# Loading q in 4352-byte runs, with q and FFN columns in blocks of 32 tokens and a new issue order, in an attention-plus-FFN kernel

## The chip, the cores and the metric

The kernel runs on one core of one Trainium2 chip. The time is the device time of that core, in microseconds (us). One number is a median over several executions. A run is called slow when it is over 1.5% above the fastest run of the same kernel; ratios use fast runs only. Engines in the profile: PE (matmul), PEld (PE's weight loads), DVE (VectorE), ACT (ScalarE), POOL (GpSimd), SP (SyncE, which issues most DMAs; a "q" after an engine name means its sequencer, where issues and waits are shown).

## The reference

Inputs are q, k, v of shape (4 batches, 4 heads, 1088 tokens, 32), small matrices S1, S2 (8 x 32), and FFN weights. All is fp32 at the interface.

```python
def phi(x):                                   # 64 features per token and head
    a = np.einsum('rd,bhsd->bhsr', S1, x)
    b = np.einsum('rd,bhsd->bhsr', S2, x)
    return np.einsum('bhsi,bhsj->bhsij', a, b).reshape(*x.shape[:-1], r * r)
q_p, k_p = phi(q), phi(k)
kv  = np.einsum('bhsf,bhsd->bhfd', k_p, v)    # one small matrix per batch and head
z   = np.sum(k_p, axis=2)
x   = (q_p @ kv) / (q_p . z + 1e-6)           # attention output, heads joined: 128 columns
# FFN on x, with the previous token mixed in
xk  = mu_k * x + (1 - mu_k) * x_prev
xr  = mu_r * x + (1 - mu_r) * x_prev
out = sigmoid(xr @ w_r) * (relu(xk @ w_k) ** 2 @ w_v)     # 128 -> 1024 -> 128
```

All K of a batch must be summed before any q of that batch can be used. So the start of the kernel is: load K and V of batch 0, sum them, fold the sum with S, then project q, then the FFN. From there on, K sums of later batches run between FFN work of earlier ones.

## The kernel before

The kernel is written as small named operations with an explicit issue order (ORDER). `KT` transposes K, `KP` projects it, `KF` makes the products kp, `KA` adds up kv on PE, `KD` folds the sum; `QT`, `Q1`, `QF`, `QR`, `QX` do the same for q; `M1`, `RE`, `SQ`, `M2` are the FFN, `FN` multiplies by the sigmoid and stores. `Z/n` are n dummy matmuls that keep PE busy. `/DVE`, `/ACT` name the engine, `/b3` the PSUM bank.

The parts that the change and the argument touch:

```python
hdq = [const.tile([P, U, 2, D], F32, name=f"hdq{b}") for b in range(B)]

def load_k(b, eng):                            # 4352-byte runs
    eng.dma_start(hdk[b][:], k[b].rearrange("h (a c u) d -> (h a) c u d", a=32, c=2))

def load_q(b, engs):                           # 4 DMAs a batch, 256-byte runs
    for h in range(H):
        engs[h % len(engs)].dma_start(hdq[b][32 * h:32 * h + 32].rearrange("a t c d -> a t (c d)"),
                                      q[b, h].rearrange("(t a c) d -> a t (c d)", a=32, c=2))
# ... all loads are issued at once on SyncE, batch by batch
load_k(0, nc.sync)
# ... S1, S2, mu_k, mu_r on ScalarE
load_v(0, nc.sync)
load_q(0, [nc.sync])
for b in range(1, B):
    load_k(b, nc.sync)
    load_v(b, nc.sync)
    load_q(b, [nc.sync])
# ... weights, on GpSimd's queue
nc.gpsimd.dma_start(wk[:], moe_w_k)
nc.gpsimd.dma_start(wr_f[:], moe_w_r)
nc.gpsimd.dma_start(wv[:], moe_w_v.rearrange("(c p) d -> p c d", p=P))

GS = [2, 2, 4, 4, 4, 4, 4, 4, 4, 2]            # groups of 128-token tiles
parts = [(0, 2), (2, n)] if n == 4 else [(0, 3), (3, n)]      # each K sum in two parts

def fin(g):                                    # one output DMA per group, 128 partitions
    n = GS[g]
    o = work.tile([P, 4, P], F32, name="osb", tag="osb", bufs=4)
    nc.vector.tensor_mul(flat(o[:, :n]), tiles[f"o_{g}"][:, :n * P], rs[g][:, :n * P])
    nc.sync.dma_start(orow[G0[g] * P:(G0[g] + n) * P].rearrange("(t p) f -> p t f", p=P), o[:, :n])
```

## Time and profile before

| | before |
|---|---|
| time, median of 3 runs | 98.54 us (97.06 to 99.57) |
| span of the profiled run (which took 97.5 us) | 95.7 us |
| first K product on DVE starts | 9.37 us |
| last product on DVE ends | 91.96 us |
| from there to the end of the span (the tail) | 3.71 us |

Lines from the page of the kernel before. The first numbers are busy time, share of the span and instruction count. The rows of digits cut the span into 40 slices: busy tenths per engine, PE's granted clock in tenths (PEclk), DMA engines' busy tenths, and GB/s. The DMA queue lines give packets, megabytes and share of the engines' time. The last of these lines is a DMA group with its issue count, size of each and time to landing.

```profile
span 95.7 us, 3103 instructions
PE 84.5 (88%) x1285; PEld 57.5 (60%) x1285; DVE 79.6 (83%) x187; ACT 69.5 (73%) x161; POOL 5.6 (6%) x24
...
PE   5969898498849999999999999999999999999920
...
DVE  4073974989278999999799999989999999999840
...
PEclk9999999999999999999999999999999999999997
DMA  2999999999999999000010300340000030030422
GB/s 66 264 226 181 226 180 199 178 232 199 202 163 250 245 181 138 10 0 0 0 55 7 110 7 0 110 116 0 0 0 0 7 98 15 0 110 0 116 83 81
DMA packets 17773, 9.70 MB, mean 101 GB/s; under 512 B 10704, under 2 KB 17104, under 8 KB 17760
...
PE 34%; DMA 22%; ACT 18%; DVE 13%; SPq 6%; issue 3%; DVEq 1%; ACTq 0%
...
hdq<-in_q_dram SPq DMA_DIRECT2D x16, 136.0 KB, 7.3
```

After slice 12 (29 us) PE and DVE are full. Before it, DVE has holes and the DMA row stands at 9 up to slice 16, 38 us. More than half the packets are under 512 bytes, most of them q. The chain of work that ended last spends 22% in DMA. The list of waits of the same kernel (engine, line, what it waited for; us in total, times, longest) names loads among the waits of VectorE:

```profile
DVE St L247 <- DMA S<-in_S_dram: 3.2, 1, 3.2
...
DVE kT L310 <- DMA hdk<-in_k_dram: 2.3, 1, 2.3
```

And the group that stores the output (durations of an issue are minimum, median and maximum in ns):

```profile
L562 SPq DMA_DIRECT2D out_dram<-osb x10: 372/372/952, 34.6 to 92.1; - x10
```

### The profile page before, as it was taken

To read this page: it belongs to the slowest core of one execution; us is meant where nothing else is said; L and a number is where in the kernel's file an instruction comes from. 1 tells how busy PE (TensorE), PEld (TensorE's weight loads), DVE (VectorE), ACT (ScalarE), POOL (GpSimd) and SP (SyncE) were. 2 spreads that over 40 slices of the span, in tenths; PEclk is the share of its full clock that TensorE was granted. 3 is DMA by queue.
4 is the path that set the end of the run, shared out by engine and by line. 5 is a ranking of instruction groups with operands and counts; after the bars stand their busy time and mean duration, and the time that the engine had idled before them with its cause. 6 is when DMAs were issued, how large, how long until landed. Compare 5 with 4: busy or idle time off the path is not lost.

```text
span 95.7 us, 3103 instructions
## 1 busy us (share of the span) xinstructions
PE 84.5 (88%) x1285; PEld 57.5 (60%) x1285; DVE 79.6 (83%) x187; ACT 69.5 (73%) x161; POOL 5.6 (6%) x24
## 2 busy tenths in 40 slices
PE   5969898498849999999999999999999999999920
PEld 1316556464637668787567588876459636748910
DVE  4073974989278999999799999989999999999840
ACT  0622101379928879899999999568999999999900
POOL 6005400050000000000000000000000000000000
PEclk9999999999999999999999999999999999999997
DMA  2999999999999999000010300340000030030422
GB/s 66 264 226 181 226 180 199 178 232 199 202 163 250 245 181 138 10 0 0 0 55 7 110 7 0 110 116 0 0 0 0 7 98 15 0 110 0 116 83 81
DMA packets 17773, 9.70 MB, mean 101 GB/s; under 512 B 10704, under 2 KB 17104, under 8 KB 17760
## 3 DMA queue, kind: packets, MB, share of 16 engines
q1 hardware_dynamic: 16224, 8.92, 45.6%
q0 software_dynamic: 1216, 0.59, 4.5%
q8 instruction: 10, 0.16, 0.7%
q10 hardware_dynamic: 320, 0.00, 0.2%
q14 instruction: 3, 0.02, 0.1%
HBM read 7.80 MB, written 2.23 MB: 105 GB/s over the span
## 4 chain that ended last, share of the span: by engine, by line
PE 34%; DMA 22%; ACT 18%; DVE 13%; SPq 6%; issue 3%; DVEq 1%; ACTq 0%
DMA hdk<-in_k_dram 15%; ACT k L515 9%; PE ps_h L507 8%; PE ps_o L536 7%; DMA hdq<-in_q_dram 6%; SPq L169 6%; PE ps_kv L345 4%; PE ps_abw L420 3%; PE ps_x L480 3%; ACT PP L489 3%; ACT k L526 3%; DVE k L524 3%; DVE XK L494 3%; PE ps_qtp L465 3%; PE ps_kab L317 2%
## 5 line engine op out<-in xcount | busy, mean ns | idle before, releaser
L515 ACT ACTIVATE k<-ps_h 128x512 bf16<-128x512 f32 (+1 forms) x66 | 32.1, 577 | 0.7 <-PE ps_h L507 0.6
L507 PE MATMUL ps_h<-XK,wk 128*128 128x512 bf16 (+1 forms) x80 | 21.6, 349 | 0.4 <-DVE k L517 0.2
L536 PE MATMUL ps_o<-wv,k 128*128 128x128 bf16 x272 | 18.9, 219 | 0.1
L536 PEld LDWEIGHTS <-k 128*128 128x128 bf16 x272 | 16.3, 98 | 3.5 <-issue 0.8
L524 DVE TENSOR_TENSOR k<-k 128x1024 bf16<-128x1024 bf16 (+1 forms) x25 | 14.8, 618 | 0.4 <-ACT k L515 0.4
L526 ACT ACTIVATE k<-k 128x1024 bf16<-128x1024 bf16 (+1 forms) x15 | 13.7, 922 | 0.0
L300 DVE TENSOR_TENSOR kp<-ab 128x512 f32<-128x512 f32 (+1 forms) x16 | 11.5, 744 | 1.5 <-ACT ab L286 1.5
L465 PE MATMUL ps_qtp<-ident,qp 128*128 128x128 f32 x68 | 9.9, 277 | 1.6 <-DVE qp L300 1.6
L300 DVE TENSOR_TENSOR qp<-an,ps_abw 128x512 f32<-128x512 f32 x17 | 11.0, 679 | 0.1
L286 ACT COPY qpT<-ps_qtp 128x512 f32<-128x512 f32 (+1 forms) x17 | 8.5, 544 | 2.1 <-PE ps_qtp L465 2.0
L465 PEld LDWEIGHTS ps_qtp<-ident,qp 128*128 128x128 f32 x68 | 7.6, 141 | 4.1 <-issue 1.5
L507 PEld LDWEIGHTS <-wk 128*128 128x128 bf16 x80 | 6.7, 97 | 5.3 <-issue 2.5
L243 PE MATMUL wt<-zero 128*128 128x512 bf16 x24 | 8.4, 498 | 1.2 <-DVE warm L156 1.2
L480 PE MATMUL ps_x<-qpT,kvS 64*32 64x512 f32 (+7 forms) x104 | 9.2, 450 | 0.0
L517 DVE TENSOR_SCALAR k<-ps_h 128x512 bf16<-128x512 f32 (+1 forms) x14 | 9.0, 642 | 0.1
L494 DVE SCALAR_TENSOR_TENSOR XK<-ps_x,mu_k,PP 128x512 bf16<-128x512 f32 (+7 forms) x13 | 7.0, 560 | 1.4 <-ACT XB L286 1.1
L310 DVE STREAM_TRANSPOSE kT<-hdk 128x256 f32<-128x256 f32 (+1 forms) x16 | 6.2, 432 | 2.3 <-DMA hdk<-in_k_dram 2.3
L317 PE MATMUL ps_kab<-SW,kT 128*64 128x64 f32 x144 | 6.1, 227 | 1.5 <-DVE kT L310 1.5
L345 PE MATMUL ps_kv<-kp,vt 128*32 128x64 f32 x288 | 6.9, 224 | 0.5 <-issue 0.3
L489 ACT ACTIVATE PP<-ps_x,omu_k 128x256 f32<-128x256 f32 (+7 forms) x12 | 6.2, 542 | 1.5 <-PE ps_x L480 1.5
L420 PE MATMUL ps_abw<-SW,qT 128*64 128x96 f32 x136 | 6.9, 250 | 0.3 <-DVE SW L288 0.3
L420 PEld LDWEIGHTS ps_abw<-SW,qT 128*64 128x64 f32 x136 | 5.8, 137 | 2.3 <-issue 1.0
(69 smaller groups left out, 100.0 us busy)
## 6 DMA issues: line engine op xcount, KB each, us to landing
hdk<-in_k_dram SPq DMA_DIRECT2D x4, 544.0 KB, 5.6
hdq<-in_q_dram SPq DMA_DIRECT2D x16, 136.0 KB, 7.3
out_dram<-osb SPq DMA_DIRECT2D x7, 256.0 KB, 2.3
vt<-in_v_dram SPq DMA_DIRECT2D x4, 288.0 KB, 8.7
vt<-in_v_dram SPq DMA_DIRECT2D x4, 256.0 KB, 7.8
out_dram<-osb SPq DMA_DIRECT2D x3, 128.0 KB, 4.5
wk<-in_moe_w_k_dram POOLq DMA_DIRECT2D x1, 256.0 KB, 10.5
wv<-in_moe_w_v_dram POOLq DMA_DIRECT2D x1, 256.0 KB, 12.9
```

The lines of the kernel that those rows point to most:

```text
L300: nc.vector.tensor_mul(o.rearrange("p t h i j -> p (t h) i j"), _ap(a_, [[sa, y], [1, R], [0, R]]), _ap(b_, [[sb, y], [0, R], [1, R]]))
L345: nc.tensor.matmul(kv[32 * h:32 * h + 32, :64], vt[b][:, h, T, :], kp[:, t, h].rearrange("p i j -> p (i j)"), start=(T == 0), stop=(T == 8 ...
L420: nc.tensor.matmul(p[64 * c:64 * c + 64, t * 96:t * 96 + 96], qT[:, s:s + 64], SW[:, s // S].rearrange("p h x r -> p (h x r)"), skip_group ...
L465: nc.tensor.transpose(p[:, t * P:t * P + P], qp[g][:, t, 2 * pair:2 * pair + 2].rearrange("p h i j -> p (h i j)"), ident[:])
L480: nc.tensor.matmul(p[D * h:D * h + D, c0:c0 + m], kvS[r:r + 64, b, D * h:D * h + D], qpT[g][r:r + 64, h // 2, c0:c0 + m], skip_group_check ...
L489: nc.scalar.activation(PP[:, c:c + m], tiles[f"x_{g}"][:, c0:c0 + m], COPY, scale=omu_k[:])
L494: nc.vector.scalar_tensor_tensor(XK[:, s:s + m], tiles[f"x_{g}"][:, c0:c0 + m], mu_k[:], PP[:, c:c + m], op0=MUL, op1=ADD)
L507: nc.tensor.matmul(h[:, :n * P], wk[:, c * P:(c + 1) * P], XK[:, G0[g] * P:(G0[g] + n) * P])
L515: nc.scalar.activation(o, i, RELU)
L524: nc.vector.tensor_mul(k2[:, :, :n * P], k1[:, :, :n * P], k1[:, :, :n * P])
L526: nc.scalar.activation(k2[:, :, :n * P], k1[:, :, :n * P], mybir.ActivationFunctionType.Square)
L536: nc.tensor.matmul(o[:, t * P:t * P + P], k2s[g, j][:, c, t * P:t * P + P], wv[:, 2 * j + c, :], start=(j == 0 and c == 0 and t == 0), sto ...
```

## The change

The intent is to make q arrive in long runs, so that the loads end sooner. A q partition then holds 34 neighbouring tokens of one head (4352 bytes), and a 32 x 32 transpose gives columns in blocks of 32 tokens that are strided over the sequence. q, x and the FFN all keep this column order, so "the previous token" is the block before, the first and last blocks of a batch need small extra work (on GpSimd), and the output rows of a group have to be stored by four or more DMAs of 32 partitions each instead of one of 128. The setup of S is shorter and half of S is now loaded over SyncE, the K sums of batches 1 to 3 are made in one part instead of two, the FFN groups are cut as 1, 2, 4, ..., 4, 3 tiles, and the issue order was searched anew. Cut to its core (GS became QS for q and FS for the FFN; some lines of ORDER stand for all of it):

```diff
-hdq = [const.tile([P, U, 2, D], F32, ...)]
+hdq = [const.tile([P, 2 * U, D], F32, ...)]
-    def load_q(b, engs):
-        for h in range(H):
-            engs[h % len(engs)].dma_start(hdq[b][32 * h:32 * h + 32].rearrange("a t c d -> a t (c d)"),
-                                          q[b, h].rearrange("(t a c) d -> a t (c d)", a=32, c=2))
+    def load_q(b, eng):
+        eng.dma_start(hdq[b][:], q[b].rearrange("h (a t) d -> (h a) t d", a=32))
# ... setup of S
-    for h in range(H):
-        nc.vector.transpose(St[D * h:D * h + D], S8[:])
-    nc.vector.tensor_mul(SW[:, 0, :, :2, :], ..., _ap(m2[:], [[1, H], [0, 2], [0, R]]))
+    nc.vector.transpose(St[:], S8[:])
+    for h in range(H):
+        (nc.vector.tensor_copy if h % 2 == 0 else nc.scalar.copy)(SW[D * h:D * h + D, 0, h, :2, :], St[:, :, :R])
# ... groups and K sums
-    GS = [2, 2, 4, 4, 4, 4, 4, 4, 4, 2]
+    QS = [2, 2, 4, 4, 4, 4, 4, 4, 4, 2]
+    FS = [1, 2, 4, 4, 4, 4, 4, 4, 4, 3]
-            parts = [(0, 2), (2, n)] if n == 4 else [(0, 3), (3, n)]
+            parts = ([(0, 2), (2, n)] if n == 4 else [(0, 3), (3, n)]) if b == 0 else [(0, n)]
# ... first and last block of a batch
+    def x_first(b):
+        nc.gpsimd.tensor_scalar(PP[:, c + 1:c + 32], XL[:, b, :31], omu_k[:], None, op0=MUL)
+        nc.gpsimd.tensor_copy(XB[:, c + 1:c + 32], XL[:, b, :31])
+        nc.gpsimd.tensor_copy(XB[:, c + S:c + XW], XL[:, b])
+    def x_end(b): ...
# ... output
-        nc.sync.dma_start(orow[...].rearrange("(t p) f -> p t f", p=P), o[:, :n])
+        for y in range(4):
+            # tiles of one batch together; two DMAs where the group spans two batches
+            for b, t, m, x in runs:
+                nc.sync.dma_start(orow[b][:, x:x + 4 * m - 3:4, :], o[32 * y:32 * y + 32, t:t + m, :])
# ... ORDER, whole
-S4T/PE/b0 S4E/ACT KT0_0/DVE KT0_1/DVE Z/3 KP0_0/PE/b0 KE0_0/ACT KP0_1/PE/b1 KF0_0_1/DVE ...
+KT0_0/DVE S4T/PE/b0 KT0_1/DVE S4E/ACT KP0_0/PE/b1 KE0_0/DVE KP0_1/PE/b0 KF0_0_1/DVE ...
```

## The prediction

> **What bounds the kernel now.** Span 95.7 us. Two regimes (busy time in ten-microsecond windows). From 30 to 90 us VectorE is busy 58.1 of 60 us and PE 59.6, ScalarE 53.7: compute, with VectorE the fullest engine (79.6 us in all; its back-to-back 512-column fp32 product costs 0.6 us, PE's modelled ends overlap, so I take VectorE as the limit). Before 30 us it is fill: VectorE idles 10.3 us. The list of waits names: weights' S load 3.2, hdk (third K batch) 2.3, the first K copy on ScalarE 1.5, the first K fold 1.2 plus 0.7 for the first q projection. After VectorE's last product (ends near 92.0) there is a 3.7 us tail of output DMA and closing. The chain of waits says the same: 15% is a K load, 6% a q load, 6% the Sync queue issuing q loads; four q issues took 7.1 and 7.2 us, so the third K load left at 16.0 and landed at 26.9. DMA engines are full until 38 us at only 160 to 260 GB/s; 10704 of 17773 packets are under 512 bytes, 8704 of them q (estimate: 2.23 MB in 256-byte runs).
>
> The Trainium skill, "DMA: Bandwidth & Descriptors", section "Why small descriptors are slow (HBM only)", puts 27% overhead on a 256-byte descriptor. This trace agrees in direction: slices with K reach 264 GB/s, those with q about 180.
>
> **What changes.**
> 1. q in 512 runs of 4352 bytes, one issue a batch. Loads should end near 28 us rather than 38, and no K, V or q wait remain on VectorE: minus 2.3 us.
> 2. Weight setup: three of four S transposes (0.23 each), a reduce and a product leave the path, and K transposes overlap it. The first K sums start near 8.0 instead of 9.4 us, the first fold about 1 us sooner.
> 3. The new order puts batch 1's K transposes and sums (about 3 us) under the first fold and projection: about minus 1.5 us of idle.
> 4. Merged K sums: six fewer VectorE fixed costs, about 0.1 us each. q transposes gain four small pieces, XK is cut a little differently; summing all instructions, VectorE goes down only 0.5 us and ScalarE 0.4. PE work is unchanged but for three dummies.
> 5. New GpSimd work (20 small instructions, about 0.2 us each) for first and last blocks; I expect it hidden, with perhaps 0.3 us lost.
> 6. Output: 52 DMAs instead of 10. An issue took 0.37 us; only those after the last product count: three more, plus 1.1 us. The last group has three tiles and nothing left to hide its second matmul: plus 0.7 us.
>
> Sum: -2.3 -1.0 -1.5 -0.5 +0.3 +1.1 +0.7 = -3.2, and about -1 from fewer small waits (XK 1.1) in the new order. Span about 91.6, time about 94.3 us (the same 2.7 us above the span as now).
>
> **What would show it.** The hdk and hdq waits gone, DMA digits 9 only to about slice 11; q issues under 1 us each; first kp product near 8 us; VectorE busy 79 us; VectorE idle before 30 us near 6 us; tail after the last product near 5 us with four output issues of 0.37 us each.
>
> **What would make it wrong.** Loads that were not limiting beyond the one wait: then order latency in the compute part takes the gain back. Output issues slower than 0.37 us for 32 partitions, or GpSimd blocks late and XK or the FFN waiting on them (slower). A better balance of VectorE and ScalarE through the search, or the tail hidden (faster). Rounds of before spread 97.1 to 99.6, so 2% is near the noise.
>
> Chances: faster by over 2% 0.86, within 2% 0.12, slower 0.02. Time 94.3 us, eight in ten between 91.8 and 96.4.

## The result, and the profile after

Measured: 99.98 us median of 4 runs (99.76 to 101.59) against 97.80 us (97.02 to 99.57, 4 runs) before. The change made the kernel slower. The ratio of fast runs is 1.0295, 95% interval 1.0252 to 1.0339. A ratio here and below is the mean time of one kernel's fast runs over the mean of the other's fast runs of the same rounds, so it is not quite the ratio of the medians that are quoted.

The same lines of the page after:

```profile
span 97.9 us, 3150 instructions
PE 82.5 (84%) x1272; PEld 56.7 (58%) x1282; DVE 79.7 (81%) x184; ACT 69.7 (71%) x166; POOL 12.7 (13%) x44
...
PE   4997891994599999899999999999999979997300
...
DVE  3189999697386989998999999997999989999200
...
PEclk9999999999859999999999999999999999999975
DMA  2799999999960012000013012113000232002351
GB/s 53 240 228 342 278 266 343 268 236 317 220 177 31 3 34 54 7 0 0 0 34 80 7 27 60 27 29 78 0 0 19 53 89 59 3 19 48 77 121 44
DMA packets 10063, 9.72 MB, mean 99 GB/s; under 512 B 2480, under 2 KB 8880, under 8 KB 10048
...
q8 instruction: 10, 0.16, 0.7%
...
PE 70%; DVE 10%; ACT 10%; issue 4%
...
hdq<-in_q_dram SPq DMA_DIRECT2D x4, 544.0 KB, 12.4
```

What was aimed at did happen: 7710 packets fewer, up to 343 GB/s, the DMA row is full up to slice 11 (27 us, with a 6 in the next) and not 16, the last load lands at 31.9 us (before 38.9), and DMA has left the chain. The front is ahead: the first K product starts at 7.53 us (before 9.37), the first fold at 12.40 (13.75). But slices 10 and 11 are weak on PE and DVE, and slices 11 and 12 have a low clock, 8 and 5. The list of waits has new entries there and one at the end:

```profile
ACT k L549 <- PE ps_h L541: 2.9, 4, 2.0
DVE k L558 <- ACT k L549: 2.8, 3, 2.3
...
PEld ps_kf L386 <- issue: 2.5, 1, 2.5
PE ps_h L541 <- issue: 2.3, 1, 2.3
...
DVE osb L595 <- PE ps_o L570: 1.4, 2, 1.0
...
DVE qT L425 <- DMA hdq<-in_q_dram: 0.9, 1, 0.9
```

"Issue" is a wait for nothing that the profile shows. Everything else then waits for PE. By windows of 1 us (busy share of each engine with instruction count, then PE's granted clock, DMA share and GB/s):

```profile
core 0: us, PE busy (x) PEld busy (x) DVE busy (x) ACT busy (x) POOL busy (x), PEclk, DMA share, GB/s
...
23.00:24.00 1.00, 0.25 (x2) 0.07 (x2) 0.83 (x3) 0.77 (x5) 0.00 (x0) 1.00 0.94 321
24.00:25.00 1.00, 0.00 (x0) 0.00 (x0) 0.00 (x0) 0.00 (x0) 0.00 (x0) 1.00 1.07 213
25.00:26.00 1.00, 0.46 (x5) 0.42 (x6) 0.00 (x0) 0.21 (x2) 0.00 (x0) 1.00 1.18 249
26.00:27.00 1.00, 1.00 (x8) 0.26 (x8) 0.90 (x3) 0.50 (x3) 0.00 (x0) 0.51 1.10 208
27.00:28.00 1.00, 1.00 (x21) 1.00 (x20) 1.00 (x5) 0.92 (x2) 0.00 (x0) 0.50 0.91 242
...
```

From 24 to 25 us nothing computes while the DMA engines are full; the clock is then halved. PE's timeline (start, length, group, and in brackets the idle time before it) shows that it stops in the middle of one and the same group of matmuls, which therefore cannot have waited for an operand that all of them share (a_warm, below, tests this):

```profile
22.37 0.88 PE L541 MATMUL ps_h<-XK,wk 128*128 128x128 bf16 x6
25.54 0.22 PE L541 MATMUL ps_h<-XK,wk 128*128 128x128 bf16 x1 [2.29 <-issue]
```

The trace's DMA records say what PE lacked. They have a queue that carries PE's own instructions (the line "q8 instruction" above: 10 packets, 0.16 MB, so 16 KB each). In the quiet part of this trace packets 7 and 8 start within 0.02 us of the moment when PE begins its 1712th and 1968th recorded instruction (matmuls, weight loads and PE's few semaphore records counted together), and packet 9 0.11 us after the 2224th, that is 256 apart. Counted back by 256, the second packet was asked for at the 432nd, at 17.16 us. It started only at 22.94 us and was in at 24.24. The view of the DMA queues has no packet of q8 from 14 to 22 us, and this one from 22 to 23 (packets, megabytes, share of the engines' time):

```profile
q8 instruction: 1, 0.02, 8.1%
```

PE had meanwhile used up all it had: its gap (2.56 us from start to start, of which the timeline counts 2.29 as idle) lies after the 703rd, about 270 instructions after the request. In the kernel before, the second packet was asked for at 19.17 and started at 22.25 us; PE had then begun only 520 and never ran dry. (Starts of packets are recorded. Which instruction triggers a request is inferred, and a few records may be missing. In other kernels the quiet packets come up to 30 counts later: in the kernel before at the 1742nd, 1987th and 2244th, which would put its request at 20.0 us. So take the times of requests as good to about 1 us.)

The Trainium skill, "Runtime: NRT & Kernel Launch", section "Instruction fetch mechanics", says that an engine's instruction memory is refilled in blocks of 16 KiB, 256 instructions, over the sequencer's own DMA queue, and that the cost is "mostly hidden". The block size agrees with this trace; here the cost was not hidden.

The half clock runs from 26.02 to 29.43 us, 3.41 us. The skill's "TensorE: Matmul & The Clock Gate", "Part 1: The HAM clock gate", states that PE's clock is set by how busy PE was, at full or half rate, over windows of 3413 ns; the length agrees. The profiled run of the kernel before had no such window until its tail, from 94.67 us. But its other fast runs, which have no trace, had mean clocks between 0.971 and 1.0 in later jobs (0.995 in the profiled one), so some of them ran longer at half clock too; where in the kernel is not recorded.

The second loss is at the end. The output group after, then the timeline of SyncE's issues:

```profile
L605 SPq DMA_DIRECT2D out_dram<-osb x52: 315/425/1507, 33.7 to 95.3; - x52
```

```profile
87.70 8.02 SPq L605 DMA_DIRECT2D out_dram<-osb  x14
```

The last product ended at 92.07 us, nearly where it had before (91.96). But SyncE was still issuing the groups before it: from 86.87 us on its last 16 issues follow each other with pauses of at most 0.45 us (read one by one in the trace; the line shows those after 88 us, merged). The last group's four issues began at 93.62, 94.04, 94.93 and 95.30, where before the last issue began at 92.12. The tail grew from 3.71 to 5.80 us. That is 2.1 of the 2.2 us by which the profiled spans differ; the lead of the front had been used up by then, by the stall and the clock as the experiments argue.

### The profile page after: what moved, and what is told of

Same layout as the page of the kernel before. It is cut to its first block, busy times and chain, and to the rows that moved or that the text cites. A ratio compares the mean times of both kernels' runs of the same rounds, so it can differ in the third digit from the quotient of the medians.

```text
span 97.9 us, 3150 instructions
## 1 busy us (share of the span) xinstructions
PE 82.5 (84%) x1272; PEld 56.7 (58%) x1282; DVE 79.7 (81%) x184; ACT 69.7 (71%) x166; POOL 12.7 (13%) x44
## 4 chain that ended last, share of the span: by engine, by line
PE 70%; DVE 10%; ACT 10%; issue 4%
PE ps_o L570 14%; PE ps_h L541 13%; PE ps_x L500 9%; PE ps_abw L440 7%; PE ps_qtp L485 6%; PE wt L246 5%; PE ps_kab L333 4%; DVE kp L316 4%; PE ps_kv L361 4%; PE ps_r L582 3%; ACT k L549 3%; ACT k L560 3%; PE ps_r L583 2%; ACT qpT L302 2%; DVE ab L304 1%
## 5 line engine op out<-in xcount | busy, mean ns | idle before, releaser
L549 ACT ACTIVATE k<-ps_h 128x512 bf16<-128x512 f32 (+3 forms) x66 | 31.7, 569 | 3.0 <-PE ps_h L541 2.9
L541 PE MATMUL ps_h<-XK,wk 128*128 128x512 bf16 (+3 forms) x72 | 19.4, 354 | 2.7 <-issue 2.3
L558 DVE TENSOR_TENSOR k<-k 128x1024 bf16<-128x1024 bf16 (+3 forms) x27 | 15.9, 605 | 2.9 <-ACT k L549 2.8
L560 ACT ACTIVATE k<-k 128x1024 bf16<-128x1024 bf16 (+2 forms) x13 | 12.1, 951 | 0.1
L316 DVE TENSOR_TENSOR kp<-ab 128x512 f32<-128x512 f32 (+3 forms) x10 | 11.0, 1114 | 0.4 <-ACT ab L302 0.4
L526 POOL TENSOR_SCALAR PP<-XL,omu_k 128x31 f32<-128x31 f32 x4 | 2.0, 498 | 52.6 <-ACT XL L302 52.6
L551 DVE TENSOR_SCALAR k<-ps_h 128x512 bf16<-128x512 f32 (+3 forms) x14 | 8.3, 608 | 0.1
L361 PEld LDWEIGHTS ps_kv<-kp,vt 128*32 128x32 f32 x288 | 4.7, 110 | 5.3 <-DVE qp L316 2.1
L595 DVE TENSOR_TENSOR osb<-ps_o,r 128x512 f32<-128x512 f32 (+3 forms) x10 | 6.0, 602 | 1.4 <-PE ps_o L570 1.4
L513 DVE SCALAR_TENSOR_TENSOR XK<-ps_x,mu_k,PP 128x512 bf16<-128x512 f32 (+8 forms) x13 | 6.8, 545 | 0.1
```

The costliest lines, as they stand in the source:

```text
L316: nc.vector.tensor_mul(o.rearrange("p t h i j -> p (t h) i j"), _ap(a_, [[sa, y], [1, R], [0, R]]), _ap(b_, [[sb, y], [0, R], [1, R]]))
L361: nc.tensor.matmul(kv[32 * h:32 * h + 32, :64], vt[b][:, h, T, :], kp[:, t, h].rearrange("p i j -> p (i j)"), start=(T == 0), stop=(T == 8 ...
L541: nc.tensor.matmul(h[:, :n * P], wk[:, c * P:(c + 1) * P], XK[:, F0[g] * P:(F0[g] + n) * P])
L549: nc.scalar.activation(o, i, RELU)
L558: nc.vector.tensor_mul(k2[:, :, :n * P], k1[:, :, :n * P], k1[:, :, :n * P])
L560: nc.scalar.activation(k2[:, :, :n * P], k1[:, :, :n * P], mybir.ActivationFunctionType.Square)
```

## The experiments

Theory A: the full load queue delays PE's second instruction packet, PE runs dry near 23 us and the clock follows; and the 52 issues lengthen the tail. Rivals: the new order or the layout is itself slower; the clock is lower for reasons that have nothing to do with the stall; the faster loads were worth nothing to begin with. Thirteen kernels ran, in four jobs, each job on one chip with its own runs of the kernel before. "The packet" is PE's second instruction packet; all results are correct unless said.

| kernel | packet asked, started (us) | PE's gap where it ran dry | half clock before the tail | last product ends, tail | ratio to before |
|---|---|---|---|---|---|
| before | 19.17, 22.25 | none | none | 91.96, 3.71 | 1 |
| after | 17.16, 22.94 | 2.56 | 26.0 to 29.4 | 92.07, 5.80 | 1.0295 |
| after_again | 18.64, 23.44 | 1.53 | 15.9 to 19.3 | 91.28, 6.35 | 1.0149 |
| a_pace | 17.16, 18.61 | none | none | 88.38, 6.21 | 0.9853 |
| a_tail | 17.43, 24.10 | 3.65 | 26.5 to 33.3 | 94.73, 3.91 | 1.0146 |
| a_warm | 16.09, 22.53 | 3.39 | 26.2 to 33.0 | 94.32, 5.9 | 1.0339 |
| a_pace3 | 16.49, 23.00 | 2.83 | 27.1 to 30.5 | 92.25, 5.7 | see below |
| a_wv | 17.99, 23.02 | 1.97 | 14.7 to 18.1 | 93.74, 6.4 | 1.0437 |
| a_pace_split | 16.72, 18.29 | none | none | 88.62, 5.9 | 0.9837 |
| a_pace_tail | 17.13, 19.10 | none | none | 88.42, 4.54 | 0.9632 |
| a_pace_tail_again | 17.45, 19.23 | none | none | 88.62, 4.5 | 0.9703 |
| a_pace_tail_wv | 16.11, 19.01 | none | none | 88.90, 4.5 | 0.9756 |
| a_pace_tail2 | 16.19, 17.96 | none | none | 87.84, 4.23 | 0.9633 |
| b_q4352 | 20.84, 24.84 | none | 9.9 to 13.3 | 91.48, 3.5 | 0.9941 |
| b_out4 | 20.06, 25.21 | none | none | 91.71, 6.06 | 1.0207 |

The profiled runs of a_tail, a_warm and a_pace3 were slow; I read from them where and why PE stops, not how long the kernel takes; the tail of a_tail is from such a run too.

### a_pace: fewer loads in the queue while the packet is wanted

Loads of batches 2 and 3 (all but K of batch 2) are issued after the first block of x exists, near 22 us. The small write makes them wait by a true dependency.

```diff
     for b in range(1, B):
-        load_k(b, nc.sync)
-        load_v(b, nc.sync)
-        load_q(b, nc.sync)
+        if b < 3:
+            load_k(b, nc.sync)
+        if b < 2:
+            load_v(b, nc.sync)
+            load_q(b, nc.sync)
# at the end of x_first(b)
+        if b == 0:
+            nc.gpsimd.memset(vt[2][:64, 0, 0, :1], 0.0)
+            load_v(2, nc.sync)
+            load_q(2, nc.sync)
+            load_k(3, nc.sync)
+            load_v(3, nc.sync)
+            load_q(3, nc.sync)
```

> The changed kernel with one edit: the loads of batch 2 (V, q) and batch 3 are issued only after the first-block work of batch 0 on GpSimd (about 22 us), so few loads stand in the DMA queues when PE's second 16 KB block of instructions is asked for. Theory A (PE ran out of instructions at 23.0 us because that block waited behind the loads, and the idle PE then lost half its clock for 3.4 us): block 2 starts within 2 us of its request instead of 5.8, no PE gap over 1 us near its 702nd instruction, granted clock 0.98 or more, time 3 to 4 us less than the changed kernel (96 to 97 us). Theory B (the new order is simply slower in the middle, the stall is one of several): the stall may go, but the time falls by less than 1.5 us. Theory C (the matmul at the stall waits for data or a weight load): stall stays.

Measured: 95.88 us (95.33 to 96.53) against 97.41 before; ratio 0.9853 (0.9756 to 0.9951). The packet was asked for at the same 17.16 us as in the changed kernel, and started 1.46 us later instead of 5.78. In the view of the DMA queues from 17.2 to 20 us:

```profile
q8 instruction: 1, 0.02, 2.8%
```

The windows show no hole and a full clock where the changed kernel stood still:

```profile
23.00:24.00 1.00, 0.94 (x10) 0.51 (x8) 0.85 (x4) 1.00 (x6) 0.00 (x0) 1.00 0.53 92
24.00:25.00 1.00, 1.00 (x24) 0.76 (x22) 1.00 (x5) 0.84 (x4) 0.00 (x0) 1.00 1.13 282
25.00:26.00 1.00, 1.00 (x19) 0.74 (x17) 1.00 (x4) 1.00 (x4) 0.00 (x0) 1.00 1.17 235
26.00:27.00 1.00, 1.00 (x24) 0.78 (x21) 1.00 (x2) 1.00 (x6) 0.00 (x0) 1.00 1.04 270
```

Where the time comes from can be read at two more places. The 688th recorded instruction of PE starts at 22.18 us after the change and at 22.03 here. The first output's product ends at 33.65 and 29.96, 3.69 us apart; the last product ends at 92.07 and 88.38, again 3.69 apart. So all but about 0.15 us of the difference arises between 22 and 34 us. The gap (2.56) and the half clock (3.41 us at half rate, at most 1.7 us of work lost, an estimate) together allow up to 4.3 us. Later loads did not cost anything that I can see. The DMA row of this kernel stays full to 33 us and its last load lands at 34.6, later than in the changed kernel (27 and 31.9 us), so their early end is not what makes it fast.

### a_tail and b_out4: the issues of the output

a_tail leaves the loads as they are and moves some issues from SyncE to other engines:

```diff
-                nc.sync.dma_start(orow[b][:, x:x + 4 * m - 3:4, :], o[32 * y:32 * y + 32, t:t + m, :])
+                eng = nc.sync
+                if g == 7 and y > 1:
+                    eng = nc.gpsimd
+                if g == 9 and y > 1:
+                    eng = nc.scalar
+                eng.dma_start(orow[b][:, x:x + 4 * m - 3:4, :], o[32 * y:32 * y + 32, t:t + m, :])
```

> The changed kernel, only the output issues of group 7 (half to GpSimd's queue) and of the last group (half to ScalarE's queue) moved off the Sync queue. Theory A (four issues a group of about 0.5 us each pile up on the Sync queue, the last group's first issue is 1.5 us late and its four take 2.1 us): tail after the last product 3.5 to 4 us instead of 5.8, time 1.8 to 2.3 us less (about 97.8). Rival (the tail is the landing and closing, not the issue): under 0.7 us less. The stall at 23 us and the clock near 0.96 stay.

Measured: 99.13 us (98.00 to 100.93), ratio 1.0146 (1.0025 to 1.0267). The tail was 3.91 us, the stall stayed, so the kernel is still slower than before. The time fell less than expected, and after_again (below), which has no edit, had the same ratio: by time alone this run resolves no gain. The pair a_pace_split and a_pace_tail (below, one job) is clearer: the last products end at 88.62 and 88.42, the tails are 5.85 and 4.54 us, the ratios 0.9837 and 0.9632. So the two losses are separate.

b_out4 does the opposite: the kernel before, with each output stored by four DMAs of 32 partitions.

```diff
-        nc.sync.dma_start(orow[...].rearrange("(t p) f -> p t f", p=P), o[:, :n])
+        dst = orow[...].rearrange("(t p) f -> p t f", p=P)
+        for y in range(4):
+            nc.sync.dma_start(dst[32 * y:32 * y + 32], o[32 * y:32 * y + 32, :n])
```

> The kernel before with each group's output sent as four transfers of 32 partitions instead of one of 128 (result unchanged). Theory A for the tail: the last two groups' eight issues of 0.45 us each follow their products, so the tail after the last product grows from 3.7 us by 2 to 2.7 us, and the time by as much (99.5). Rival (issues are free, landing decides): under 0.7 us.

Measured: 100.42 us (99.59 to 101.25) against 98.97; ratio 1.0207 (1.0110 to 1.0303). The last product ends at 91.71, the last issue starts at 95.05, and the tail is 6.06 us.

```profile
L564 SPq DMA_DIRECT2D out_dram<-osb x40: 315/431/1382, 34.2 to 95.0; - x40
```

An issue takes 431 ns in the median, against 372 for a whole group before, and there are four times as many. The loss of the tail belongs to the number of issues, without any other part of the change.

### a_warm: asking for the packet earlier

Eight dummy matmuls (16 recorded instructions) before the K sums of batch 1. PE reaches its 432nd instruction earlier, while it waits for V of batch 1 anyway.

```diff
-... QP1/DVE KE1_1/ACT QP1/DVE KA1_0_0/PE/b7 QD0/DVE ...
+... QP1/DVE KE1_1/ACT QP1/DVE Z/8 KA1_0_0/PE/b7 QD0/DVE ...
```

> The changed kernel with 8 warming matmuls (16 instructions) put where PE idles from 14.9 to 17.1 us, before the second batch's first K sums. Theory A: PE asks for instruction block 2 about 2 us sooner (its 431st instruction is reached near 15 us instead of 17.2), so the stall is shorter by up to 2 us, and what is left of it sits at the same instruction number 702, thus 16 instructions earlier in the program (among the first FFN matmuls rather than at the seventh); time 1 to 3 us less. Theory C (a wait of the one matmul for its data): the stall stays at that matmul with its length. Rival for the clock (missing warm-up work, not the stall): clock 0.99 even though the stall stays.

Measured: 101.65 us (100.15 to 102.45), ratio 1.0339 (1.0191 to 1.0488). My expectation fell: by the count the packet was asked for 1.07 us earlier than in the changed kernel, and it still started at 22.53. If the request was earlier, it only waited longer. But the run answers another question, because the program is shifted: PE stopped again after its 705th recorded instruction, and the matmul that it could not start is now another one, of the sigmoid branch, about 16 instructions earlier in the program.

```profile
25.21 0.23 PE L582 MATMUL ps_r<-wr_c,XB 128*128 128x128 bf16 x1 [3.17 <-issue]
```

The stall keeps its count, not its operation. No operand of the matmul at which it stops can be the cause.

### b_q4352: the fast q load alone, in the kernel before

```diff
-        for h in range(H):
-            engs[h % len(engs)].dma_start(hdq[b][32 * h:32 * h + 32].rearrange("a t c d -> a t (c d)"), ...)
+        engs[0].dma_start(hdq[b][:].rearrange("p t c d -> p (t c) d"), q[b].rearrange("h (a t) d -> (h a) t d", a=32))
```

The result is wrong (tokens are permuted, relative error 1.41); the work is the same.

> The kernel before with only the q load changed to one transfer a batch in runs of 4352 bytes; the tokens of q come out permuted, so the result is wrong on purpose, the work is the same. If the q form alone was worth what I predicted: the 2.3 us wait for the third K batch goes, time 1.5 to 3 us less than before (95 to 96). If faster loads by themselves bring the instruction stall: a PE gap over 1.5 us at an instruction number near 446, 702 or 958, and no gain or a loss. Theory A says the stall needs the PE to be ahead of its instruction blocks, which the order of before is not, so a gain is expected.

Measured: 97.11 us (96.05 to 98.35) against 97.41; ratio 0.9941 (0.9771 to 1.0110). The wait for the third K batch is gone from the list, as the prediction had it, but a gain is not resolved, where 1.5 to 3 us had been expected. Part of it went back at once, to the load of the small matrix S, which came later: the wait for it grew from 3.2 to 4.5 us,

```profile
DVE St L245 <- DMA S<-in_S_dram: 4.5, 1, 4.5
```

and the first K product started at 10.99 us instead of 9.37. The packet started late here too (24.84), but PE had asked for it late (20.84) and was not dry: in these runs PE ran dry only where faster loads came together with a front that is ahead. A front that is ahead with the old loads was not run.

### a_pace_tail, and the same with wv later

a_pace_tail has both edits, a_pace and a_tail. a_pace_tail_wv also issues the load of wv (the second FFN matrix, 256 KB in the profile, in the small packets of GpSimd's queue) after the first block.

> Both edits together: late loads of batches 2 and 3, and output issues of group 7 and of the last group spread over two queues. Theory A: the gains add, 4 us (loads) and about 2 us (tail), so 93.5 to 94.5 us, 3 to 4% below the kernel before; tail after the last product under 4 us, no PE gap near instruction 702. If the two overlap or the tail gain of the single run came from elsewhere: 95 us or more.

> As a_pace_tail, with the load of the second FFN weight also moved behind the first-block work (about 22 us). PE's remaining gap of 1.7 us at 15 to 17 us waits for the V load of batch 1 (landed at 17.0 us in the changed kernel). If that load is late because of the bytes ahead of it, it lands about 1 us sooner, the gap shrinks to under 1 us and the time falls by 0.3 to 1 us. Rival: one DMA engine straggles whatever stands ahead: no change; and if the weight arrives too late for the first second-layer matmul (about 28 us): slower by up to 2 us.

Measured: a_pace_tail 94.55 us (93.81 to 95.08, 6 runs) against 98.97; ratio 0.9632 (0.9564 to 0.9700). The last product ends at 88.42, as in a_pace, and the tail is 4.54. a_pace_tail_wv: 96.00 us (94.98 to 96.72), ratio 0.9756 (0.9676 to 0.9837), slower. Its wait for V of batch 1 was shorter (gap of PE 1.05 against 1.54 us), but the first K product began 0.64 us later and the last ended 0.48 us later. What makes the rest of the difference is not settled.

### a_pace_split: the merged K sums undone

```diff
-            parts = ([(0, 2), (2, n)] if n == 4 else [(0, 3), (3, n)]) if b == 0 else [(0, n)]
+            parts = [(0, 2), (2, n)] if n == 4 else [(0, 3), (3, n)]
# ORDER: KF1_0_0/DVE -> KF1_0_0/DVE KF1_0_1/DVE, KA1_0_0/PE/b7 -> KA1_0_0/PE/b7 KA1_0_1/PE, and so on
```

> a_pace with the merged K sums of batches 1 to 3 undone (each product and its matmuls in two parts again, at the same places in the order). The merge saves six VectorE instructions' fixed cost: VectorE busy up by 0.6 to 0.9 us, time up by 0.3 to 1 us against a_pace (96.2 to 96.9). If the merge was worth nothing, or cost latency: equal or faster than a_pace.

Measured: 96.53 us (96.04 to 97.06), ratio 0.9837 (0.9742 to 0.9933), beside 0.9853 for a_pace in another job. VectorE is busy 79.6 us against 79.5. The merging of the K sums gave nothing that these runs resolve.

### after_again, a_pace3: how much has to be held back

after_again is the changed kernel without an edit, to see how far stall and clock repeat. a_pace3 holds back batch 3 alone:

```diff
-        load_k(b, nc.sync); load_v(b, nc.sync); load_q(b, nc.sync)
+        if b < 3:
+            load_k(b, nc.sync); load_v(b, nc.sync); load_q(b, nc.sync)
# at the end of x_first(0)
+            nc.gpsimd.memset(hdk[3][:, 0, 0, :1], 0.0)
+            load_k(3, nc.sync); load_v(3, nc.sync); load_q(3, nc.sync)
```

> The changed kernel again, unedited, so that the edits stand beside it on one chip. If the stall belongs to the kernel and not to one profiled execution: a PE gap of 2 us or more at its 702nd to 705th instruction, granted clock 0.95 to 0.98, about 100 us, 2 to 3.5% above the kernel before. If it was a chance of that chip: no gap, clock 0.99, 96 us.

> A smaller dose of the late loads: only batch 3 is held back until about 22 us, batch 2 is issued early as in the changed kernel. If a block of instructions waits for the loads that stand queued when it is asked for (Theory A), then block 2, asked for at 17.2 us, starts between the 18.6 us of the larger dose and the 22.9 us of none, estimate 20 to 21 us (the 5 MB of three batches at about 280 GB/s, with the weights); that is before PE runs out at 23 us, so no gap over 1 us, clock 0.98 or more, 96 to 97 us. If queued loads don't matter: start near 23 us and the gap as in the changed kernel.

Measured: after_again 99.62 us (98.36 to 99.84) against 98.44; ratio 1.0149 (1.0044 to 1.0255). The stall is there, 1.53 us, at the same count; it is shorter because PE came to its 432nd instruction later (18.64). Its half-clock window, however, lies before the stall (15.9 to 19.3 us). So the stall is not the only thing that halves the clock in this kernel, and the link between them in the first trace is likely but not shown. Over the six kernels that ran dry, a half-clock window follows the four gaps of 2.56 us and more, and none follows the two of 1.53 and 1.97 us.

a_pace3: 100.20 us (97.41 to 100.78); three of its four runs were slow, the one fast run took 97.41, so no ratio is given. My expectation fell: the packet started at 23.00, no earlier than with all loads in the queue, and PE was dry for 2.83 us. Batch 2's V and q were still under way: they landed between 22.2 and 25.9 us. To hold back batch 3 alone is not enough.

### a_pace_tail_again, a_pace_tail2: the version to keep

a_pace_tail2 is a_pace with a simpler tail: three of the last group's four stores go from ScalarE, nothing from GpSimd.

```diff
+                eng = nc.scalar if g == 9 and y > 0 else nc.sync
+                eng.dma_start(orow[b][:, x:x + 4 * m - 3:4, :], o[32 * y:32 * y + 32, t:t + m, :])
```

> The kernel with both edits, repeated on another chip beside the changed kernel: 93.8 to 95 us, 3 to 4.5% below the kernel before, 5 to 6% below the changed one.

> As a_pace_tail, but GpSimd's queue issues no output; three of the last group's four issues go to ScalarE's queue, one stays on the Sync queue. In a_pace_tail 2.1 us passed between the last landing and the end of the span, in the kernel before 1.3: if GpSimd's output transfers cause this, the end comes about 0.8 us sooner after the last landing, while the last issue is about 0.6 us later; so equal within 0.5 us of a_pace_tail. If not, 0.5 to 1 us slower than a_pace_tail.

Measured: a_pace_tail_again 95.07 us (94.34 to 95.89), ratio 0.9703 (0.9639 to 0.9768); a_pace_tail2 94.20 us (93.58 to 95.06), ratio 0.9633 (0.9556 to 0.9710). Lines of the page of a_pace_tail2:

```profile
span 92.1 us, 3163 instructions
...
DVE  4098979999999899979999999997999989999510
...
PEclk9999999999999999999999999999999999999997
DMA  2889999911999951000031022022000124001263
```

The hole in VectorE's row (slice 11 after the change) is gone, and the DMA row shows where the queue now has a pause (slices 9 and 10). The span ends 0.9 us after the last landing, where in a_pace_tail it ended 2.1 us after it. a_pace_tail2 is 3.7% faster than the kernel before, with all of the change's parts in it (95% interval 2.9 to 4.4%). The two intervals overlap, so which of the two tails is the faster one is not resolved; by the record's rule a_pace_tail_again is faster than before, and a_pace_tail2 is left at unclear.

### a_wv: which of the queued loads holds the packet up

One rival was left. In the changed kernel the last packet of wv, on GpSimd's queue, starts at 22.16 us, 0.8 us before the instruction packet, and it is near it in other traces as well. a_wv moves wv alone:

```diff
-    nc.gpsimd.dma_start(wv[:], moe_w_v.rearrange("(c p) d -> p c d", p=P))
# at the end of x_first(0)
+            nc.gpsimd.memset(wv[:, 0, :1], 0.0)
+            nc.gpsimd.dma_start(wv[:], moe_w_v.rearrange("(c p) d -> p c d", p=P))
```

> The changed kernel with nothing held back but the FFN's second weight matrix wv (576 KB in small packets on GpSimd's queue), which is now issued after the first block's work, near 22 us. In the changed kernel PE's second instruction packet was asked for at about 17.2 us, started at 22.94 us, 0.8 us after wv's last packet had started (22.16); in the kernel before 0.65 us after it. Theory A (the K, V and q loads of the Sync queue hold the packet up): they are still queued without a break until about 25 us, so the packet still starts at 21 to 24 us, PE still runs dry near its instruction 704 for 1.5 us or more, and a half-clock window still follows; ratio to the kernel before 1.01 to 1.03. Rival B (wv's packets in the second queue hold it up): the packet starts within 3 us of being asked for, by about 20 us, PE does not run dry, and the ratio is about 0.99, like the kernel with the later loads held back (0.985).

Measured: 101.53 us (100.77 to 102.05) against 97.38; ratio 1.0437 (1.0344 to 1.0529). The packet started at 23.02, with no packet of GpSimd's queue having started since 14.7 us, and PE ran dry in the same place:

```profile
23.15 0.80 PE L543 MATMUL ps_h<-XK,wk 128*128 128x128 bf16 x6
25.65 0.22 PE L543 MATMUL ps_h<-XK,wk 128*128 128x128 bf16 x1 [1.70 <-issue]
```

So wv is not the cause; of the loads tested that leaves the K, V and q loads of SyncE's queue, and holding those back did end it (a_pace). (The expectation gives wv 576 KB; that is what all three weights on GpSimd's queue come to, wv is 256 KB.) Two parts of the expectation fell. No half-clock window follows the stall. And the ratio is worse than theory A had it; wv now arrives late and the FFN waits for it:

```profile
PE ps_o L572 <- DMA wv<-in_moe_w_v_dram: 2.8, 1, 2.8
```

## Why the prediction was wrong, point by point

The prediction said 94.3 us, 91.8 to 96.4, and 0.86 for faster by over 2%. The kernel took 99.98 us.

1. "Loads should end near 28 us rather than 38, and no K, V or q wait remain on VectorE: minus 2.3 us." The first half was right: the DMA row is full only to 27 us and the 2.3 us wait on K is gone. A q wait of 0.9 us remained. The step that failed is the credit: it counted faster loads as pure gain. b_q4352 had the same q load for a ratio of 0.9941, not told apart from 1. Nothing in the sum stood for what else has to pass through the same DMA engines. With SyncE's queue full and the compute ahead (PE's 432nd instruction at 17.16 instead of 19.17 us), PE's second instruction packet waited 5.78 us and PE was dry for 2.56 us. This term is missing from the sum altogether, and with the clock it is worth 3.69 us (last product 92.07 after the change, 88.38 in a_pace).
2. Weight setup: right in size, and in part by luck. The first K product started at 7.53 us (predicted near 8.0), the fold 1.35 us sooner (predicted about 1). But 0.6 us of it is a shorter wait for S (3.2 before, 2.6 after), which the prediction did not count; half of S now goes over SyncE.
3. The new order: right in kind. VectorE's idle time before 30 us was predicted near 6 us; it is 10.3 before, 7.8 after the change and 5.3 in a_pace. The stall hid it.
4. Merged K sums, -0.5: no gain resolved (a_pace_split).
5. GpSimd, +0.3: no wait of VectorE, ScalarE or PE for a GpSimd block is in the list of waits, so nothing was lost that shows.
6. Output, "only those after the last product count: three more, plus 1.1 us": mis-sized. The tail grew by 2.1 us. Issues that were thought hidden were not: the last 16 follow each other almost without a pause from 86.87 us, and the last group's first one began 1.55 us after its product had ended. The issue itself took 0.425 us in the median and not 0.37. The last group's exposed second matmul cost 1.0 us of waiting where 0.7 was foreseen.
7. "About -1 from fewer small waits" was not worked out from anything. The prediction implied a last product near 86.6 us (span 91.6 less a tail of 5). With the stall taken away, it ended at 88.38 and 87.84. So some 1.2 to 1.8 us of the gain had been claimed too much, even without the two losses.
8. "The same 2.7 us above the span as now" compared a median with the span of another run. The profiled run of before took 97.5 us for a span of 95.7, 1.8 us more; this moved the prediction 0.9 us too high.

Together these terms account for the miss. The profiled run took 99.86 us, 5.6 more than predicted: 3.7 for the stall and the clock, 1.8 for gains claimed too much, 0.8 for a tail of 5.8 instead of 5.0, less 0.7 because this run lay 2.0 us above its span and not 2.7.

The prediction named a general risk, that "order latency in the compute part takes the gain back". That is not what happened: the order is kept in the version that is 3.7% faster. Its other risk, output issues slower than 0.37 us, did come true (0.425 us), but is the smaller part. It gave this outcome a chance of 0.02, too little for a change with 52 instead of 10 stores and a wholly new order.

What stays open: how the DMA engines choose between the instruction packet and the loads. In every kernel with an unbroken load queue the packet started between 22.25 and 25.21 us, whenever it had been asked for (16.09 to 20.84), though loads were still running then. In the six kernels that ran dry it started 0.6 to 1.2 us before one and the same load landed, the second V transfer of batch 2, which SyncE had issued at 8.8 to 10.3 us. That fits a packet which keeps its place behind loads that were issued long before, and it would explain why holding back batch 3 alone did nothing; but it is not tested, and the request may be earlier than my count says. And whether the stall halves the clock, or idle time of PE from earlier does, was not separated.

## What to carry to other kernels

A load queue that is always full can delay more than the next load: in this kernel PE's instructions came through the same DMA engines and waited 5.78 us, and the faster front used its instructions sooner. When PE stands still with "issue" as the reason, count its instructions and look for the instruction packets in the DMA records, then hold back loads that are not needed yet. When stores are cut into more pieces, count the issues from the last point at which the issuing queue was empty, and spread the last ones over other engines.

## What the Trainium skill lacked or had wrong

- "Runtime: NRT & Kernel Launch", "Instruction fetch mechanics": it calls the cost of crossing a 16 KiB block "mostly hidden" and does not say that running loads can delay the block. Here it waited 5.78 us while they ran, PE was dry for 2.56 us, and holding loads back (a_pace) brought the wait to 1.46 us. The section also gives PE an instruction memory of 2048 instructions. In six kernels PE ran dry after its 703rd to 705th recorded instruction, some 270 after it had asked for a block, so the instructions that were at hand were far fewer than 2048; a note in the same section that the memory is two lines of 16 KiB fits this better.
- "DMA: Bandwidth & Descriptors", "Queues, rings and completion order": it says that each DMA engine goes round robin between queue rows packet by packet. By that one would expect a lone packet in its own row to start soon; in the kernels here with an unbroken load queue the second instruction packet waited 3.1 to 6.7 us by the count. What it waits for, no run shows, so this is a question to the page and not a proof against it.
- The same page, "Issuing engines are not separate DMA queues": issuing from several engines saves only the sequencer's time, "which is usually small relative to the DMA itself". At the end of this kernel it was not small: four issues of about 0.43 us for a group of stores that land 1.7 us after issue. Moving three of the four to ScalarE shortened the tail from 6.21 us (a_pace) to 4.23 (a_pace_tail2).
